# Gate and up weight forms of an fp32r feed-forward block at 28 different byte offsets in their places

## The chip, the cores and the metric

The kernel runs on one core of one Trainium2 chip. The metric is the device time of one execution in microseconds (us), smaller is better; for each kernel the median of its runs is given. The profile shows one execution, engine by engine: PE is TensorE's matmuls, PEld its weight loads (LDWEIGHTS, which overlap the matmuls), DVE is VectorE, ACT is ScalarE, POOL is GpSimd, SP is SyncE, which issues all the DMAs here.

## The reference

Input x has 2048 tokens of 512 features, all fp32. The result is x + s * g, with

```
xn = layernorm(x)
q, k, v = split(xn @ wqkv)                 # 32 heads of 16
phi(t) = where(t > 0, t + 1, exp(t)) + 1e-6
kv = sum over tokens of phi(k) v^T ; z = sum over tokens of phi(k)
s = ((phi(q) kv) / (phi(q) z + 1e-6)) @ wo
g = silu((gelu(xn @ w_gate) * (xn @ w_up)) @ w_down)
```

with w_gate and w_up 512 x 1792 and w_down 1792 x 512. The change touches how the weights of xn @ w_gate and xn @ w_up lie in SBUF.

## The kernel before, in words

Every fp32 product is made of three fp32r matmuls (mm3, lines 291 to 295): each operand is split into a high form, rounded to fp32r on ACT, and a low form, the rest, made on DVE (split, lines 287 to 289). Line 293 is stationary high by moving high, line 294 stationary high by moving low, line 295 stationary low by moving high. The PE therefore sees long rows of matmuls that each have 128 stationary columns, loaded by an LDWEIGHTS of their own, and 512 moving columns. The products are cut further by a seven-product scheme of the Strassen-Winograd kind: of each pair of 256-wide blocks seven products are made from sums of weights and sums of tokens (PRODUCTS, line 24).

The work has these stages in order of time: layernorm, transposes and the k and q products (to about 145 us of the span); the first half of the feed-forward, tokens 1024 and up (about 145 to 400 us, with kv and the matrix M made inside it and at its end); the attention output S, which is spread over the row of matmuls that follows; the second half of the feed-forward (to about 610 us); and the last products and outputs.

In the feed-forward there are 28 groups of weights, q = 0 to 27: 14 for the first half of the tokens and the same 14, prepared again, for the second; even q are gate blocks, odd q are up blocks. `prep_w(q)` (lines 687 to 709) loads a 512 KB block, forms sums of it on POOL (tmp) and writes 14 slices of 128 x 128 as high forms and 14 as low forms into one tile w of the pool "wp" (ACT writes the high ones, DVE the low ones). The pool has four places, used in turn (`sl = w_next[0] % 4`), each 28 x 128 fp32 numbers = 14,336 bytes in every partition. The places are used before that by the k and q weight forms KQ (line 346) and in between by the two forms M_hi and M_lo of the matrix M (lines 901 to 904). `fprod` (lines 713 to 723) multiplies: the stationary operand is a 128-column slice of w (tile names w), the moving one 512 columns of the token forms Xh or Xl (tiles of pool "xf", line 328). The seven products of a group go to PSUM tiles FX, FY and FZ, 42 matmuls in a group, 1,176 in all. The down products (tiles d, line 785 on) take token forms hh and hl as stationary operand and down-weight forms dwh and dwl as moving one; they do not read w.

The order of the work is written out by a planner (class Plan): PE's order is a list of keys made by hand, and each of the other engines' orders follows from costs and due times given in the code. It knows nothing of addresses. Pools are laid out in SBUF one after another: constants, xf, wp, rawp, dp, up, sm. In the built program before the change, xf starts at byte 5,248 of each partition, wp at 62,592, and the two SBUF operands of every matmul stand at a distance that is a multiple of 512 bytes.

Of the kernel before, what the change touches and what calls it, by code (L numbers as in the profile page):

```python
# [9 lines left out]
F32R = mybir.dt.float32r  # L10
# [4 lines left out]
P = 128  # L15
# [179 lines left out]
def kernel(  # L195
# [35 lines left out]
    def tile_in(pool_name, unit, shape, dtype, name, parts=1):  # L231

        gen = gens[pool_name, unit] = Gen(gens.get((pool_name, unit)))
        kept = []

        def get():
            if not kept:
                kept.append(pools[pool_name].tile(shape, dtype, name=name, tag=f"{pool_name}{unit}", bufs=1))
            return kept[0]
        return View([Res() for _ in range(parts)], get, gen, pool_name == "ps")  # L240
# [3 lines left out]
    def ring(tag, places):  # L244
        n = count[tag] = count.get(tag, -1) + 1
        return places[n % len(places)]
# [24 lines left out]
    def ext(ap):  # L271
        return View((), lambda: ap)

    def dma(dst, src, kb, name=""):
        do("SP", 0.1, lambda o, i: nc.sync.dma_start(o, i), dst, src, lat=2.3, kb=kb, name=name)
# [7 lines left out]
    def tt(eng, op, dst, a, b, n, name=""):  # L283
        e, c = (nc.vector, dve(n)) if eng == "DVE" else (nc.gpsimd, pool(n))
        do(eng, c, lambda o, p, q: getattr(e, f"tensor_{op}")(o, p, q), dst, a, b, name=name)  # L285

    def split(hi, lo, src, n, name="", eng="DVE"):
        copy("ACT", hi, src, n, name + "h")
        tt(eng, "sub", lo, src, hi, n, name + "l")
# [52 lines left out]
    def raw_tile(i, name, shape):  # L342
        return tile_in("rawp", i, shape, F32, name, 2)
# [255 lines left out]
    for n in range(NP):  # L599
# [5 lines left out]
        for i in range(2):  # L605
# [3 lines left out]
            if n < CL:  # L609
                if i:  # L610
                    b = tile_in("up", 19 + n, [P, 2, 2, P], F32R, f"b12_{n}", 2)
# [71 lines left out]
    ws = {}  # L683
# [3 lines left out]
    def prep_w(q):  # L687

        u, i = divmod(q % NQ, 2)
        rname = ring("raw", [R0, R1])  # L690
        raw = raw_tile(rname, f"raw{q}", [P, KT, 2 * P])
        dma(raw, ext((up_k if i else gate_k)[:, :, u * 2 * P:(u + 1) * 2 * P]), 512)
        sl = w_next[0] % 4
        w_next[0] += 1
        w = ws[q] = tile_in("wp", sl, [P, 2, 14, P], F32R, f"w{q}", 4)
        tmp = raw_tile(TMP, f"tmp{q}", [P, 8, P])

        def t(i, n=1):
            return tmp.part((tmp.res[i // 2],), (slice(None), slice(2 * i, 2 * (i + n))))
        a11, a21 = raw[:, 0:2, 0:P], raw[:, 0:2, P:]  # L700
        a12, a22 = raw[:, 2:4, 0:P], raw[:, 2:4, P:]
        tt("POOL", "add", t(0), a21, a22, 256, "S1")
        tt("POOL", "sub", t(1), t(0), a11, 256, "S2")
        tt("POOL", "sub", t(2), a11, a21, 256, "S3")
        tt("POOL", "sub", t(3), a12, t(1), 256, "S4")
        for g, src in enumerate((raw[:, :, 0:P], a22, t(0, 2), t(2, 2))):
            n = (GROUPS[g].stop - GROUPS[g].start) * P
            hv, lv = (w.part(w.res[g:g + 1], (slice(None), hl, GROUPS[g])) for hl in range(2))
            split(hv, lv, src, n, f"w{g}")
# [103 lines left out]
    def ffn(p, finish):  # L813
        base = 0 if p else NQ
        todo = [list(g) for g in groups]
        for u in range(NU):
            for i in range(2):
                q = base + 2 * u + i
                if q not in ws:
                    prep_w(q)  # L820
                quad(q, p)
            prep_d(p, u)
            if todo[0][-1] == u:
                g = todo.pop(0)
                down(p, g, g is None or g[0] == 0, not todo, finish)
# [75 lines left out]
    for nm in ("M_hi", "M_lo"):  # L901
        sl = w_next[0] % 4
# [119 lines left out]
```

## Time and profile before

| | |
|---|---|
| time before, median of 2 runs | 638.58 us (637.63 to 639.53) |
| time of the profiled execution | 640.52 us |
| its span, first to last instruction | 638.8 us |
| granted TensorE clock, mean | 0.994 of full speed |
| matmuls in the trace | 2,772, each with its weight load |
| of them with w as operand | 1,176 |

The page of the profile shows the busy time of each engine, the span in 40 slices, the DMA queues, the chain of work that ended last, and groups of instructions by source line, engine, operation and tile, with count, busy time and mean duration of one. A matmul's duration in the trace is longer than the distance to the next one, since matmuls are pipelined: the distance between the starts of neighbours (the pitch) is what adds up to time. The timeline lists instructions with start, duration and the idle time before them; the view by windows gives, for stretches of the span, each engine's busy time and its number of instructions.

### The profile page before, as it was taken

How to read it: one execution, taken by the hardware profiler on the slowest of the kernel's cores; microseconds unless marked ns; L12 is line 12 of the kernel's file. 1: busy time of each engine (PE TensorE's matmuls, PEld its weight loads, DVE VectorE, ACT ScalarE, POOL GpSimd, SP SyncE). 2: the span in 40 equal slices, each digit the busy share in tenths (PEclk: the TensorE clock that was granted, in tenths of full speed). 3: DMA queues.
4: the chain of work that ended last, by engine and by line, in shares of the span. 5: the costliest groups of instructions: out<-in, count | busy, mean ns of one | idle time of the engine just before them, and what ended most of it. 6: DMA issues, size and time to landing. Idle time of an engine off the chain costs nothing.

```text
span 638.8 us, 7793 instructions
## 1 busy us (share of the span) xinstructions
PE 620.2 (97%) x2772; PEld 506.8 (79%) x2772; DVE 418.5 (66%) x634; ACT 323.2 (51%) x571; POOL 261.8 (41%) x253
## 2 busy tenths in 40 slices
PE   6999899999999999999999999999999999999995
PEld 5787678888888888888887788878888888888884
DVE  5889778768866664673266787866666537733564
ACT  5667577777765641561255132256656316612431
POOL 3552654445554652352016245455546403510144
PEclk8999999999999999999999999999999999999998
DMA  6248830105323211111149444773222201101154
GB/s 230 92 126 238 267 103 33 67 34 158 106 66 100 56 48 37 60 42 58 34 140 352 183 174 139 266 237 93 68 65 67 67 24 43 33 1 33 34 190 139
DMA packets 52439, 68.66 MB, mean 107 GB/s; under 512 B 2864, under 2 KB 31792, under 8 KB 52400
## 3 DMA queue, kind: packets, MB, share of 16 engines
q1 hardware_dynamic: 52400, 68.17, 33.0%
q8 instruction: 21, 0.34, 0.2%
q14 instruction: 18, 0.15, 0.1%
HBM read 49.28 MB, written 18.87 MB: 107 GB/s over the span
## 4 chain that ended last, share of the span: by engine, by line
PE 86%; DMA 4%; DVE 4%; ACT 2%; issue 1%; POOL 1%; SPq 0%; DVEq 0%; ACTq 0%; POOLq 0%
PE FX L293 8%; PE FX L294 8%; PE FX L295 8%; PE d L295 7%; PE d L294 7%; PE d L293 7%; PE FZ L294 4%; PE FZ L295 4%; PE FZ L293 4%; PE sps L295 2%; PE sps L293 2%; PE sps L294 2%; PE FY L294 2%; PE FY L295 2%; PE FY L293 2%; PE gps L294 2%
## 5 line engine op out<-in xcount | busy, mean ns | idle before, releaser
L763 POOL TENSOR_TENSOR h<-h,g 128x512 f32<-128x512 f32 x42 | 63.2, 1506 | 164.0 <-DVE h L285 163.8
L293 PE MATMUL FX<-Xh,w 128*128 128x512 f32 x224 | 87.6, 391 | 0.2
L293 PE MATMUL d<-dwh,hh 128*128 128x512 f32 x224 | 87.8, 392 | 0.0
L294 PE MATMUL FX<-Xl,w 128*128 128x512 f32 x224 | 87.2, 389 | 0.0
L295 PE MATMUL d<-dwh,hl 128*128 128x512 f32 x224 | 87.2, 389 | 0.0
L295 PE MATMUL FX<-Xh,w 128*128 128x512 f32 x224 | 87.2, 389 | 0.0
L294 PE MATMUL d<-dwl,hh 128*128 128x512 f32 x224 | 87.1, 389 | 0.0
L285 POOL TENSOR_TENSOR tmp<-raw 128x256 f32<-128x256 f32 x56 | 47.9, 856 | 85.1 <-DVE w L285 62.4
L801 DVE TENSOR_TENSOR acc<-acc,d 128x512 f32<-128x512 f32 (+1 forms) x49 | 32.9, 674 | 58.1 <-PE d L295 58.1
L279 ACT COPY fu<-FX 128x512 f32<-128x512 f32 x56 | 32.9, 587 | 58.9 <-PE FX L295 58.8
L285 DVE TENSOR_TENSOR hl<-h,hh 128x512 fp32r<-128x512 f32 x56 | 53.4, 974 | 4.6 <-ACT hh L279 4.4
L279 ACT CAST hh<-h 128x512 fp32r<-128x512 f32 x56 | 34.5, 620 | 41.7 <-PE d L294 21.7
L293 PEld LDWEIGHTS FX<-Xh,w 128*128 128x128 f32 x224 | 42.0, 188 | 10.2 <-ACT fu L279 1.5
L285 DVE TENSOR_TENSOR w<-tmp,w 128x512 fp32r<-128x512 f32 x56 | 41.4, 754 | 13.3 <-ACT w L279 13.3
L294 PEld LDWEIGHTS d<-dwl,hh 128*128 128x128 f32 x224 | 42.1, 188 | 8.9 <-issue 0.2
L293 PEld LDWEIGHTS d<-dwh,hh 128*128 128x128 f32 x224 | 42.1, 188 | 8.9 <-issue 0.2
L295 PEld LDWEIGHTS d<-dwh,hl 128*128 128x128 f32 x224 | 42.0, 188 | 8.7
L295 PEld LDWEIGHTS FX<-Xh,w 128*128 128x128 f32 x224 | 42.1, 188 | 8.7
L294 PEld LDWEIGHTS FX<-Xl,w 128*128 128x128 f32 x224 | 42.1, 188 | 8.6
L293 PE MATMUL FZ<-Xh,w 128*128 128x512 f32 x112 | 43.6, 389 | 0.0
L294 PE MATMUL FZ<-Xl,w 128*128 128x512 f32 x112 | 43.6, 389 | 0.0
L295 PE MATMUL FZ<-Xh,w 128*128 128x512 f32 x112 | 43.6, 389 | 0.0
(186 smaller groups left out, 1402.2 us busy)
## 6 DMA issues: line engine op xcount, KB each, us to landing
raw<-in_B_w_gate SPq DMA_DIRECT2D x14, 512.0 KB, 3.8
raw<-in_B_w_up SPq DMA_DIRECT2D x14, 512.0 KB, 3.8
draw<-in_B_w_down SPq DMA_DIRECT2D x14, 512.0 KB, 3.4
x<-in_A_x SPq DMA_DIRECT2D x16, 256.0 KB, 3.0
q_d<-qp SPq DMA_DIRECT2D x16, 256.0 KB, 2.0
q<-q_d SPq DMA_DIRECT2D x16, 256.0 KB, 2.8
xh_d<-Xh SPq DMA_DIRECT2D x4, 896.0 KB, 5.4
xl_d<-Xl SPq DMA_DIRECT2D x4, 896.0 KB, 7.4
```

Source lines behind the costliest of these rows:

```text
L279: do("ACT", act(n), lambda o, i: nc.scalar.copy(o, i), dst, src, name=name)
L285: do(eng, c, lambda o, p, q: getattr(e, f"tensor_{op}")(o, p, q), dst, a, b, name=name)
L293: nc.tensor.matmul(ps, wh, mh, start=start, stop=False, skip_group_check=on)
L294: nc.tensor.matmul(ps, wh, ml, start=False, stop=False, skip_group_check=on)
L295: nc.tensor.matmul(ps, wl, mh, start=False, stop=stop, skip_group_check=on)
L763: do("POOL", pool(NC), lambda o, i: nc.gpsimd.tensor_mul(o, o, i), h, g, name="h")
L801: do("DVE", dve(D // n), lambda o, i: nc.vector.tensor_add(o, o, i), acc[p, j][cl], ps[cl], name="acc")
```

## The change

The tile of a group becomes one flat row of 28 x 128 + 116 numbers (14,800 bytes), and the group's forms begin 4 x (q + 1) numbers, that is 16 x (q + 1) bytes, into it: 16 bytes for q = 0, 448 for q = 27. The view that the rest of the code sees has the shape it had before.

```
-        w = ws[q] = tile_in("wp", sl, [P, 2, 14, P], F32R, f"w{q}", 4)
+
+        off = 4 * (q + 1)
+        w = ws[q] = tile_in("wp", sl, [P, 28 * P + 116], F32R, f"w{q}", 4).map(
+            lambda ap: ap[:, off:off + 28 * P].rearrange("p (a b c) -> p a b c", a=2, c=P))
```

In the built program each place of wp takes 14,816 bytes (pools give out whole 32-byte units), 480 more than before. So places 1, 2 and 3 start 480, 960 and 1,440 bytes later, and the pools behind wp (rawp, dp, up, sm) 1,920 bytes later; xf does not move. Both programs hold the same instructions in the same order with the same waits on every engine; what differs is addresses, and line numbers below line 695, which are 3 higher after the change. Taken modulo 512 bytes, the distance from the token forms Xh and Xl to the weight forms is 0 for all 28 groups before. After the change it is 16 + 16q plus 480 for each place before the group's own: 16, 0, 496, 480, 80, 64, 48, 32, 144, 128, 112, 96, 208, 192 for q = 0 to 13 and 240, 224, 208, 192, 304, 288, 272, 256, 368, 352, 336, 320, 432, 416 for q = 14 to 27. For even q it is an odd multiple of 16, for odd q a multiple of 32. The KQ forms in places 1 to 3 (480, 448 and 416 modulo 512 from Xh and Xl), the pair M and pqT, and the operands in pool "up" that meet Xh, Xl or KQ change their distance too; the down products and the sums over tokens (gps) do not, since both their operands move together.

## The prediction

> **What bounds the kernel now.** I read the page first, then the groups of PE's instructions, then busy time by windows, the list of who PE waited for, and last the timeline, for the distance between single matmuls.
>
> ```profile
> span 638.8 us, 7793 instructions
> PE 620.2 (97%) x2772; PEld 506.8 (79%) x2772; DVE 418.5 (66%) x634; ACT 323.2 (51%) x571; POOL 261.8 (41%) x253
> PE   6999899999999999999999999999999999999995
> PEclk8999999999999999999999999999999999999998
> PE 86%; DMA 4%; DVE 4%; ACT 2%; issue 1%; POOL 1%; SPq 0%; DVEq 0%; ACTq 0%; POOLq 0%
> ```
>
> PE is busy from end to end at full granted clock, and the chain that ended last is 86% PE. The windows say how closely, in the two stretches that hold nearly all of the feed-forward:
>
> ```profile
> core 0: us, PE busy (x) PEld busy (x) DVE busy (x) ACT busy (x) POOL busy (x), PEclk, DMA share, GB/s
> 160.00:350.00 190.00, 189.95 (x838) 156.68 (x836) 114.54 (x156) 93.02 (x166) 78.34 (x76) 1.00 0.28 89
> 400.00:620.00 220.00, 219.85 (x978) 181.38 (x977) 128.84 (x184) 99.63 (x174) 82.18 (x77) 1.00 0.26 84
> ```
>
> In the first, 838 matmuls fill 189.95 of 190 us: 226.7 ns each, with no wait. What a matmul here gains or loses reaches the end of the kernel one to one; what other engines gain or lose does not, as long as PE stays fed. So the question is whether the addresses change those 226.7 ns. The matmuls that read w are these, 672 + 336 + 168 = 1,176 of them:
>
> ```profile
> L293 PE MATMUL FX<-Xh,w 128*128 128x512 f32 x224 | 87.6, 391 | 0.2
> L294 PE MATMUL FX<-Xl,w 128*128 128x512 f32 x224 | 87.2, 389 | 0.0
> L295 PE MATMUL FX<-Xh,w 128*128 128x512 f32 x224 | 87.2, 389 | 0.0
> L293 PE MATMUL d<-dwh,hh 128*128 128x512 f32 x224 | 87.8, 392 | 0.0
> ...
> L293 PE MATMUL FZ<-Xh,w 128*128 128x512 f32 x112 | 43.6, 389 | 0.0
> ...
> L293 PE MATMUL FY<-Xh,w 128*128 128x512 f32 x56 | 21.8, 389 | 0.0
> ```
>
> FZ and FY have three such rows each. The mean of one (389 ns) is its time through the pipeline, not the pitch; the pitch is read from starts in the timeline:
>
> ```profile
> 547.90 0.39 PE L293 MATMUL FY<-Xh,w 128*128 128x512 f32 x1
> ...
> 550.40 0.39 PE L295 MATMUL FX<-Xh,w 128*128 128x512 f32 x1
> ```
>
> These are 12 matmuls, so 2.50 us / 11 = 227 ns, in agreement with the window. The down products d, whose operands lie in quite other tiles, go at the same pitch; here are the first and the last of 22:
>
> ```profile
> 230.79 0.39 PE L293 MATMUL d<-dwh,hh 128*128 128x512 f32 x1
> ...
> 235.55 0.39 PE L293 MATMUL d<-dwh,hh 128*128 128x512 f32 x1
> ```
>
> 4.76 us / 21 = 227 ns.
>
> **The change, part by part.**
>
> *Instructions.* None is added, removed or moved, on no engine and no queue: order, waits and DMAs are those of before. No step has a new predecessor, so nothing can become late unless an instruction gets longer.
>
> *The matmuls with w.* Before, every operand pair of the program is a multiple of 512 bytes apart. So no row shows a pitch at another distance modulo 512. What can be read is whether the pitch holds a term that could depend on it. For the pure stream of 512 columns the nearest row is the plain fp32 product pm, each of whose four calls runs as two passes:
>
> ```profile
> L907 PE MATMUL pm<-mstuff 128*128 128x512 f32 x8 | 3.6, 592 | 0.0
> 358.13 3.59 PE L907 MATMUL pm<-mstuff 128*128 128x512 f32 x8
> ```
>
> Eight passes whose last takes 0.59 us give (3.59 - 0.59) / 7 = 429 ns of pitch. If a plain fp32 pass streams at half the fp32r rate (my assumption; it makes the two nearly commensurate), the bare stream is 429 / 2 = 214 ns, and the 227 ns hold 12 ns on top, though each of those passes has a weight load too. So about 12 ns of each fp32r matmul go with loading weights beside a stream at full rate. One reading is a meeting of the two reads in SBUF, which could depend on distance; another is a fixed cost of the swap, which could not. For the upper side, the nearest rows are matmuls just after a wait of PE, when load and stream stand in another phase to each other:
>
> ```profile
> 58.58 0.50 PE L293 MATMUL X<-kq,Xh 128*128 128x512 f32 x1 [0.24 <-ACT u L279]
> 58.92 0.40 PE L294 MATMUL X<-kq,Xh 128*128 128x512 f32 x1
> ...
> 60.31 0.39 PE L294 MATMUL Y<-kq,Xh 128*128 128x512 f32 x1
> ...
> 61.23 0.39 PE L295 MATMUL Y<-kq,Xl 128*128 128x512 f32 x1
> ...
> 62.59 0.39 PE L295 MATMUL Z<-kq,Xl 128*128 128x512 f32 x1
> ```
>
> From 58.92 to 60.31 six pitches take 1.39 us, 232 ns each; from 61.23 to 62.59 six take 1.36 us, 227 again. So the term isn't a constant of the instruction: it moves by 5 ns on average with phase, and then locks. The first pitch here, 0.34 us, holds a late load; as nothing delays loads in the change, I don't take it as an end.
>
> The bounds for the 1,176 matmuls with w are then 214 and 232 ns: 1,176 x (214 - 226.7) = -14.9 us, and 1,176 x (232 - 226.7) = +6.2 us. Between them I take 226.7, so 0. The reason is the row that it is nearest to: the pitch is the same for FX, FY, FZ and d, whose tiles lie in many different places, and it comes back to 227 ns after each disturbance; a lock that is found again from any phase may be found again from any distance, which shifts the phase of the lines read as a late start does. This is an argument, and no measurement at another distance stands behind it.
>
> The Trainium skill, "TensorE: Matmul & The Clock Gate", section "Part 2: What happens when you issue a matmul", says that PE has two independent SBUF read ports, and that loading the next weights takes no read bandwidth from the running matmul; by it the distance is worth nothing, 0 us. The same page's section "Wait — 56ns, not 53.3ns?" gives 215.7 ns for the warm pitch at 512 columns; the trace's 226.7 differs by 11.0 ns, and if that were a collision that the shift removes, an estimate by the page's figure is 1,176 x 11.0 = 12.9 us saved. The page's two statements together leave the 11 ns unexplained, and no run here shows yet which gives way.
>
> *The other matmuls whose distance changes.* With KQ, M, and tiles of "up" against X: X 144, Y 36, Z 72, k 48, q 48 and sps 192, together 540 of 512 columns. By the same two bounds they are worth 540 x (-12.7) = -6.9 us to 540 x 5.3 = +2.9 us; taken 0 for the same reason. In the first stage PE also waits now and then, so part of either end would be lost in waits. The d and gps products keep their distances: 0.
>
> *Writing and reading w on ACT and DVE.* The forms now start 16 bytes off a 32-byte unit in even groups. No row of before has such a tile, so I bound by the cover.
>
> ```profile
> L279 ACT CAST w<-raw x56: 390/507/626, 136.6 to 554.1; 128x512 fp32r<-128x512 f32 x28, 128x256 fp32r<-128x256 f32 x28
> L279 ACT CAST w<-tmp x56: 604/617/627, 143.0 to 558.8; 128x512 fp32r<-128x512 f32 x56
> L285 DVE TENSOR_TENSOR w<-raw,w x56: 410/681/1517, 137.4 to 557.2; 128x512 fp32r<-128x512 f32 x28, 128x256 fp32r<-128x256 f32 x28
> L285 DVE TENSOR_TENSOR w<-tmp,w x56: 676/684/1794, 145.2 to 559.6; 128x512 fp32r<-128x512 f32 x56
> L295 PE MATMUL FZ<-Xh,w x112: 388/389/389, 155.1 to 609.9; 128*128 128x512 f32 x112
> ```
>
> A group takes four such writes on DVE (about 0.68 us each, 2.7 us) and four on ACT (0.51 and 0.62 us, 2.3 us). On PE a group takes 42 matmuls and its share of the down products, 672 / 28 = 24, together 66 x 226.7 ns = 15.0 us; by the first window DVE is busy for 114.54 / 190 = 60% of that, 9.0 us, and ACT for 49%, 7.3 us. So DVE has 6.0 us and ACT 7.7 us to spare in a group. The last write starts at 559.6 us and the last matmul with w at 609.9 us, so the forms are also made well ahead. Writes 1.5 times as long would add 1.4 us on DVE, which is hidden: 0. The cover is gone when the writes take over 6.0 / 2.7 + 1 = 3.2 times as long; at 4 times it is 8.1 - 6.0 = 2.1 us in a group, 28 x 2.1 = +59 us. Below 0 it can't be, since a shorter write has nobody waiting for it on PE.
>
> *Sum.* 0 + 0 + 0 against the profiled execution's 640.5 us (span 638.8 and 1.7 around it). That execution is 1.9 us above the median of the two runs, 638.58, of which the higher is 639.53; the median is what I carry over: **638.6 us**.
>
> **The rivals.**
>
> *Slower: other distances meet more often.* If the 12 ns are meetings of load and stream in SBUF, and the distance 0 modulo 512, with both starting together, is a good one, then the 27 groups that leave it pay. For it speaks that the pitch can be 232 for six matmuls in a row in another phase; against it that PE locks back to 227. At 232 ns in all matmuls with w it is +6.2 us, 644.8; with the 540 others +9.1 us, 647.7; at twice that surplus +18 us, 657. A loss of 2% (12.8 us) needs 12.8 / 1,176 = 10.9 ns on average on each matmul with w, or a pitch of 238 ns; from there it decides against "no change".
>
> *Faster: the old distance is the bad one.* All operands a multiple of 512 bytes apart and load and stream started together would be the worst case of a scheme that spreads addresses over banks, and the constant 12 ns its price. Then 27 of 28 groups (one comes back to 0 modulo 512) gain up to 12.7 ns: 1,134 x 12.7 = 14.4 us, 624.2; if half of the distances gain, 631.4; with the 540 others at best about 617. For it speaks that the surplus appears in every fp32r matmul and that all of them share the distance; against it that load and stream run on different addresses of moving rows, so that a shift by a few lines need not part them, and that phase, which does the same, made it only worse in the rows above.
>
> *Slower: the forms are written more slowly* on ACT or DVE off a 32-byte unit. From 3.2 times on it decides; 59 us at 4 times. Nothing in the profile speaks for so large a factor.
>
> **How the numbers follow.** About 2% is what a measurement of this kernel can tell from no change: 12.8 us, so faster is below 625.8 and slower above 651.4.
> - No dependence that adds up, my forecast: chance 0.56, 636 to 641.5 us, all within 2%.
> - More meetings: 0.24, spread from 642 to 660 and beyond; 0.11 of it above 651.4, 0.05 above 655.
> - Fewer meetings: 0.16, from 617 to 635; 0.05 of it below 625.8.
> - Slow writes: 0.04, all above 655.
>
> So faster 0.05, slower 0.11 + 0.04 = 0.15, within 2% 0.80. The range from 626 to 655 leaves out 0.05 below and 0.05 + 0.04 above, 0.14 together; the likeliest case's own range is 636 to 641.5.
>
> **What would show it.** Right: in the first window still about 838 matmuls in 190 us with PE waiting for nothing, the pitch 227 ns in groups of every distance, and w's writes on ACT and DVE at 0.62 and 0.68 us. Wrong: a pitch that differs from group to group while d keeps 227 ns (distance matters; the sign tells which rival), with even and odd groups apart if the 32-byte unit is what counts; a changed pitch of X, Z or sps; or PE waits on ACT w or DVE w, with those writes two or more times as long.

## The result and the profile after

The changed kernel takes 645.95 us (median of 2 runs, 645.88 to 646.03) against 638.58 before: a ratio of 1.0102, 95% interval 1.007 to 1.0135, so about 7.4 us or 1% slower. The two profiled executions, 640.52 and 646.03 us, differ by 5.5, since the one before was 1.9 us above its median. From the page of the profile after:

```profile
span 644.3 us, 7793 instructions
PE 628.2 (98%) x2772; PEld 507.5 (79%) x2772; DVE 421.1 (65%) x634; ACT 323.2 (50%) x571; POOL 261.5 (41%) x253
PEclk9999899999999999999999999999999999999999
L293 PE MATMUL FX<-Xh,w 128*128 128x512 f32 x224 | 88.7, 396 | 0.1
L294 PE MATMUL FX<-Xl,w 128*128 128x512 f32 x224 | 88.3, 394 | 0.0
L293 PE MATMUL d<-dwh,hh 128*128 128x512 f32 x224 | 87.8, 392 | 0.0
L295 PE MATMUL d<-dwh,hl 128*128 128x512 f32 x224 | 87.2, 389 | 0.0
```

PE is still the bound, with the same 2,772 matmuls and the same granted clock, and is 8 us longer busy. The groups show where: the matmuls with w went from 389 to 394 ns (391 to 396 in line 293), the down products d stayed at 389 to 392. The windows show that no wait came in; the columns are those of the same view before:

```profile
160.00:350.00 190.00, 189.96 (x826) 154.66 (x825) 112.76 (x153) 91.94 (x164) 76.54 (x75) 1.00 0.26 83
400.00:620.00 220.00, 219.90 (x966) 178.81 (x966) 127.09 (x183) 99.86 (x174) 80.55 (x77) 1.00 0.25 82
```

In the first stretch 826 matmuls instead of 838 fill the same 190 us. With 24 down products at 226.7 ns to 42 matmuls with w, 230.0 ns on average means about 232 ns for those with w. The timeline shows that it isn't the same for all groups. The first pair of lines is the first and last of 18 matmuls of group 2, at distance 496 modulo 512, the second the first and last of 17 of group 10, at distance 112:

```profile
171.97 0.39 PE L293 MATMUL FX<-Xh,w 128*128 128x512 f32 x1
...
175.83 0.40 PE L295 MATMUL FX<-Xh,w 128*128 128x512 f32 x1
...
282.72 0.39 PE L293 MATMUL FX<-Xh,w 128*128 128x512 f32 x1
...
286.45 0.39 PE L294 MATMUL FX<-Xl,w 128*128 128x512 f32 x1
```

3.86 us / 17 = 227 ns in the one, 3.73 / 16 = 233 ns in the other. Summing the distances between starts of all matmuls by output tile, FX, FY and FZ took 267.4 us before and 273.3 after, +5.9 us; all others together changed by -0.3 us. That makes +5.5, as the spans show.

The groups give a first map. At 0 and 496 the pitch is 227 ns, at 256 it is 227 wherever the row had settled, and at most other distances 230 to 234. Groups 256 bytes apart show the same patterns: at 80 as at 336 it goes 230, 235, 230, 235, at 112 as at 368 it stays at 233 and 234. One group will matter later: group 8, at 144 bytes, goes at 233.4 ns over its whole length. The writes of w did not change:

```profile
L279 ACT CAST w<-tmp x56: 602/617/628, 142.3 to 563.4; 128x512 fp32r<-128x512 f32 x56
L285 DVE TENSOR_TENSOR w<-tmp,w x56: 677/685/1786, 144.6 to 564.4; 128x512 fp32r<-128x512 f32 x56
```

The medians of 617 and 685 ns are within 1 ns of those before, although half of the groups lie 16 bytes off a 32-byte unit.

### The profile page after: what moved, and what is told of

The parts are those of the page before. It is cut to its first block, busy times and chain, and to the rows that moved or that the text cites. A ratio compares the mean times of both kernels' runs of the same rounds, so it can differ in the third digit from the quotient of the medians.

```text
span 644.3 us, 7793 instructions
## 1 busy us (share of the span) xinstructions
PE 628.2 (98%) x2772; PEld 507.5 (79%) x2772; DVE 421.1 (65%) x634; ACT 323.2 (50%) x571; POOL 261.5 (41%) x253
## 4 chain that ended last, share of the span: by engine, by line
PE 89%; DVE 4%; DMA 4%; ACT 2%; issue 0%; POOL 0%; SPq 0%; ACTq 0%; DVEq 0%
PE FX L293 8%; PE FX L294 8%; PE FX L295 8%; PE d L293 7%; PE d L294 7%; PE d L295 7%; PE FZ L294 4%; PE FZ L293 4%; PE FZ L295 4%; PE sps L293 2%; PE sps L295 2%; PE sps L294 2%; PE gps L294 2%; PE gps L295 2%; PE FY L294 2%; PE FY L295 2%
## 5 line engine op out<-in xcount | busy, mean ns | idle before, releaser
L293 PE MATMUL FX<-Xh,w 128*128 128x512 f32 x224 | 88.7, 396 | 0.1
L295 PE MATMUL FX<-Xh,w 128*128 128x512 f32 x224 | 88.2, 394 | 0.0
```

Of the source, the lines that this page charges most:

```text
L293: nc.tensor.matmul(ps, wh, mh, start=start, stop=False, skip_group_check=on)
L295: nc.tensor.matmul(ps, wl, mh, start=False, stop=stop, skip_group_check=on)
```

## The experiments

The theory to test was *distance*: the pitch of an fp32r matmul hangs on the distance, modulo 256 bytes, between the weights that are loaded and the tokens that stream. The rivals were *layout* (larger places, moved pools), *place* (where w lies by itself) and *alignment* (any step off the old grid). All times are compared with runs of the kernel before on the same chip, 638.7 to 639.0 us.

**pad_only: larger places, nothing shifted.**

```
-        w = ws[q] = tile_in("wp", sl, [P, 2, 14, P], F32R, f"w{q}", 4)
+        off = 0
+        w = ws[q] = tile_in("wp", sl, [P, 28 * P + 64], F32R, f"w{q}", 4).map(
+            lambda ap: ap[:, off:off + 28 * P].rearrange("p (a b c) -> p a b c", a=2, c=P))
```

> Places of the pool wp are 256 bytes larger, all forms begin at byte 0 of them; every operand pair stands at a distance that is 0 modulo 256 bytes (0 or 256 modulo 512). Theory distance (the pitch hangs on the distance between the weights that are loaded and the tokens that stream, with a period of 256 bytes, since in the changed kernel groups 256 bytes apart had the same pitch patterns): pitch 226.7 ns in all groups, time as before, 638.6 us within 1. Theory layout (larger places and pools that moved cost it): pitch 227 but some us more, up to the 7.4 us of the change. Theory 512 (the period is 512): the two groups of places in four at 256 go at 231 to 234 ns, +3 to +4 us.

639.2 us, ratio 1.0009 (0.9998 to 1.0019). From its windows:

```profile
160.00:350.00 190.00, 189.01 (x833) 155.88 (x831) 114.64 (x157) 92.65 (x165) 78.34 (x76) 1.00 0.28 89
```

189.01 / 833 = 226.9 ns, though half of the groups stand at 256 modulo 512. Larger places cost nothing, and 256 is as good as 0.

**all_96: all groups 96 bytes into their places.** As pad_only with `off = 24`.

> As pad_only, but all 28 groups begin 96 bytes into their places, a distance at which the changed kernel showed 234 ns. Theory distance: 234 ns in all groups, 1,176 x 7.3 ns = +8.6 us, about 647.2. If the 234 came from the change of distance from group to group, or from the first stage and M, which now stand at 0: 227 ns, about 638.6.

647.77 us, ratio 1.0139 (1.0115 to 1.0162): +9.0 us where +8.6 was expected. The mean pitch between matmuls with w is 234.2 ns. Its second window:

```profile
400.00:620.00 220.00, 219.95 (x961) 178.09 (x960) 126.45 (x182) 98.69 (x172) 80.86 (x77) 1.00 0.25 81
```

961 matmuls instead of 978 in 220 us, and PE is full: the time is in the matmuls, with all other pairs at 0.

**x_moved_96: the same distance, made by moving X.** As all_96, with 160 bytes more ahead of X, so that w is back at its old place modulo 256 and X has moved.

```
     ones = const("ones", [P, P])
+    pad = const("pad", [P, 40])
+    do("DVE", 0.1, lambda o: nc.vector.memset(o, 0.0), pad)
```

> As all_96, but everything behind the first constant moved by 160 bytes, so that the forms stand at the places modulo 256 bytes that they had before the change and the token forms X moved instead; the distance is 96 again, all other pairs at 0. Theory distance: as all_96, 234 ns and about 647.2 us. Theory place (the load is slower from addresses off 128 modulo 256): 227 ns, about 638.6.

647.5 us, ratio 1.0136 (1.0121 to 1.0151), mean pitch 234.2 ns. Group 5 runs through the same pitches as in all_96, number by number: 231, 234, 235, 234, 231, 238, 237, again and again. Place falls: w lies where it lay before the change, and the cost is that of all_96.

**low_96: the low weight forms alone moved by 96 bytes.**

```
+        w = ws[q] = tile_in("wp", sl, [P, 28 * P + 64], F32R, f"w{q}", 4).map(
+            lambda ap: ap[:, 0:28 * P + 48].rearrange("p (a b) -> p a b", a=2)[:, :, 0:14 * P]
+            .rearrange("p a (b c) -> p a b c", c=P))
```

> As pad_only, but the low weight forms alone stand 96 bytes further, the high ones at 0. Two of three matmuls then have weights at 0 (lines 293 and 294), one has them at 96 (line 295). Theory next load (the load of the next weights meets the stream that runs): the pitch from a 294 to its 295 grows by about 7 ns, the pitch from a 295 to the next 293 stays at 227; 392 x 7.3 = +2.9 us, 641.5. Theory own weights (a matmul is slower with its own weights at another distance): the pitch from 295 to 293 grows instead, the same time. If the lock as a whole is lost, all three grow, up to +8.6 us.

647.72 us, ratio 1.0132 (1.0096 to 1.0168), with the four runs spread from 644.3 to 649.4. The pitches after lines 293, 294 and 295 are 233.2, 231.6 and 232.7 ns: all three grow, the one after 294 least. One matmul in three at a bad distance takes the whole row out of its steady pattern; by the sum of starts the matmuls with w cost 6.6 us more, against 8.6 in all_96. Which two reads meet, this does not tell.

**probe: the map in steps of 4 bytes.** Extra rows of 14 matmuls (stationary `lo`, streaming `h`, 512 columns, nothing else on PE), ahead of the product z, whose bank they use.

```
+        def row(s, m, rows=P, n=14):
+            for _ in range(n):
+                nc.tensor.matmul(o[0:rows, 0:m.shape[-1]], s, m, start=True, stop=True)
+        for c in range(68):
+            row(lo[:, c:c + P], h)
+        for rows in (64, 32):
+            for c in (0, 24):
+                row(lo[:, c:c + rows], h, rows)
+        for cols in (384, 256):
+            for c in (0, 24):
+                row(lo[:, c:c + P], h[:, 0:cols])
...
+        for c in range(0, 68, 4):
+            row(b[:, 512 + c:512 + c + P], b[:, 0:512])
```

> The kernel before, with rows of 14 extra matmuls at one place in the middle (ahead of the product z, whose bank they use and which overwrites them), each row at one distance and with nothing else on PE between: 68 rows with the weights moved by 0, 4, 8, ... 268 bytes against 512 streaming columns; rows with 64 and 32 weight columns and with 384 and 256 streaming columns at 0 and 96 bytes; a row that alternates 0 and 96; and 17 rows in bf16 at steps of 8 bytes. The times of the whole mean nothing. Theory distance: 226.7 ns at 0 and 256 bytes (and at 240, 16 bytes before the period), 231 to 235 ns at the others, whatever the engines beside do. If the whole excess over the bare stream is a meeting of load and stream, fewer weight columns shorten it in proportion (64 columns: from 13 to about 7 ns at 0), and some distance under 16 bytes might go below 226.7; if the 13 ns at distance 0 are a fixed cost of the swap, they stay with 64 and 32 columns, and with 384 and 256 streaming columns. Bf16 moves half the bytes in the same time: by the meeting theory less excess or none, under 3 ns, with little dependence on distance.

From its timeline, merged, come the later matmuls of the rows at 0, 144, 212 and 256 bytes, then 64 and 32 weight columns (at 96 and 0 bytes), 384 streaming columns (at 96), 256 (at 0 and at 96), and bf16 at 8 bytes; the columns are start, time to the last one's end, and count:

```profile
343.20 2.66 PE L887 MATMUL pz<-zh,zl 128*128 128x512 f32 x11
...
460.25 2.66 PE L887 MATMUL pz<-zh,zl 128*128 128x512 f32 x11
...
515.16 3.00 PE L887 MATMUL pz<-zh,zl 128*128 128x512 f32 x12
...
550.70 2.90 PE L887 MATMUL pz<-zh,zl 128*128 128x512 f32 x12
...
567.04 2.66 PE L887 MATMUL pz<-zh,zl 128*64 128x512 f32 x11
...
570.00 2.94 PE L887 MATMUL pz<-zh,zl 128*32 128x512 f32 x12
...
578.99 2.07 PE L887 MATMUL pz<-zh,zl 128*128 128x384 f32 x11
...
581.50 1.24 PE L887 MATMUL pz<-zh,zl 128*128 128x256 f32 x9
...
582.70 1.69 PE L887 MATMUL pz<-zh,zl 128*128 128x256 f32 x13
...
594.57 2.54 PE L887 MATMUL pz<-bf 128*128 128x512 bf16 x11
```

With one matmul's own 0.39 us taken off (0.34 and 0.28 for the shorter streams, 0.38 in bf16) and divided by the count less one, the pitches are, to about 1 ns, 227, 227, 237, 228, 227, 232, 173, 120, 118 and 216 ns. The whole map, as the mean of the last nine pitches of each row, by distance in bytes:

```
  0: 226.7   4: 232.4   8: 230.7  12: 230.7  16: 233.6  20: 233.3  24: 231.1  28: 235.0
 32: 233.2  36: 234.6  40: 233.3  44: 229.6  48: 233.2  52: 233.3  56: 233.3  60: 230.1
 64: 233.0  68: 233.3  72: 233.3  76: 233.7  80: 231.7  84: 235.1  88: 233.3  92: 233.2
 96: 233.9 100: 226.7 104: 233.3 108: 230.1 112: 233.3 116: 233.3 120: 226.7 124: 231.9
128: 233.8 132: 228.1 136: 232.8 140: 233.4 144: 226.7 148: 233.0 152: 231.1 156: 226.7
160: 233.3 164: 235.2 168: 233.8 172: 235.6 176: 229.9 180: 232.9 184: 231.9 188: 233.3
192: 228.9 196: 233.0 200: 230.4 204: 226.7 208: 231.8 212: 236.4 216: 232.2 220: 233.4
224: 233.4 228: 226.7 232: 231.1 236: 231.7 240: 226.7 244: 226.7 248: 233.3 252: 226.7
256: 226.7 260: 232.4 264: 230.7 268: 230.7
```

Three things follow. The rows at 260, 264 and 268 run through the very pitches of 4, 8 and 12, one by one: the period is 256 bytes. The other engines have no part in it: from 470 to 590 us DVE, ACT and POOL did nothing, and the figures at 16, 96 and 112 bytes are those of the groups in the changed kernel. And for 128 weight columns and 512 streaming ones 226.7 ns is a floor, not one value among many: eleven distances reach it, none goes below. Steady rows of 512, 384 and 256 columns take 226.7 (at 0 bytes), 173.3 (at 96) and 120.0 ns (at 0), 53.3 ns per 128 columns and 13.4 ns over. But these 13.4 ns are not a floor for every shape: 256 columns at 96 bytes go at 117.6 ns, 2.4 below the steady row at 0. The excess does not shrink with the weights, although the loads do:

```profile
L887 PEld LDWEIGHTS pz<-zh,zl 128*128 128x128 f32 x1036 | 192.3, 188 | 43.0
L887 PEld LDWEIGHTS pz<-zh,zl 128*64 128x64 f32 x28 | 3.8, 134 | 2.6
L887 PEld LDWEIGHTS pz<-zh,zl 128*32 128x32 f32 x28 | 3.0, 108 | 3.4
```

With 64 weight columns the row still goes at 227 ns at 96 bytes and 229 at 0, with 32 columns at 230 and 232. That a part of the 13 ns is in proportion to the lines loaded has fallen. With 64 weight columns it is 96 bytes that settles at the floor, and 0 does not: which distances are good depends on the shape too, so the map is one for 128 by 512. A row that alternates 0 and 96 bytes goes at 230 ns on average, 229 and 231 in turn. In bf16 the pitch is 216 ns at all 17 distances (four gaps are twice that, where the trace lacks a matmul); there distance counts for nothing.

**all_144 and all_212: does the map hold in the kernel?** As pad_only with `off = 36` and `off = 53`.

> All 28 groups begin 144 bytes into their places, other pairs at 0. Theory distance, as the probe mapped it (226.7 ns at 144 bytes from the first matmul of the row on): 227 ns in all groups, time as before, 638.8 us within 1.5. Theory alignment (any shift off the old layout costs 5 to 8 ns, and the probe's rows without other engines at work don't carry over): 231 to 235 ns, 644 to 648.

639.39 us, ratio 1.001 (1.0 to 1.0021); mean pitch with w 227.5 ns. That mean hides two patterns. Most groups go at 226.6 to 226.7 ns throughout. But after short waits of PE, near the end of group 13 and in group 14, the matmuls with w went on in a cycle of 231 to 238 ns, stayed in it through groups 15 and 16, and came back to 226.7 in group 17, after a stretch of down products. Here are the first and the last of 39 matmuls in it:

```profile
441.98 0.40 PE L293 MATMUL FX<-Xh,w 128*128 128x512 f32 x1
...
450.85 0.39 PE L295 MATMUL FZ<-Xh,w 128*128 128x512 f32 x1
```

8.87 us / 38 = 233.4 ns, with the tiles, the distance and the stream's start of the rows at 226.7. It is also what group 8 of the changed kernel, at 144 bytes, showed. So one distance can have two steady patterns, and the row changed between them at breaks; by the sum of starts that cost 0.8 us here. In pad_only, at 0 and 256, every row came back to 226.7 after its breaks, within about a dozen matmuls.

> All 28 groups begin 212 bytes into their places, the distance with the longest pitch in the probe, 236.4 ns. Theory distance by the map: 1,176 x 9.7 ns = +11.4 us, about 650.2. Theory that any bad distance costs the same in the kernel: as at 96 bytes, +8.6 to +8.9, about 647.5.

650.49 us, ratio 1.0181 (1.0163 to 1.0199); mean pitch 236.4 ns, the probe's number. Its first window holds 814 matmuls for 838 before:

```profile
160.00:350.00 190.00, 189.96 (x814) 152.71 (x813) 109.94 (x150) 90.77 (x162) 74.75 (x75) 1.00 0.25 77
```

The map predicted both, 638.8 and 650.2, within 0.6 us. Alignment falls: 144 bytes off the old grid is nearly as good as 0.

**places_480: the change without the shift of w against X.** Places as in the change, `off = 8 * sl`.

> The change without its part: places and pools where the change puts them, but each group's forms begin 0, 32, 64 or 96 bytes into its place, so that weights and tokens stand at 0 or 256 modulo 512 again. KQ against X, M against pqT and the pairs with tiles of the pool up keep the distances of the change. Theory distance in the 1,176 alone: back to 638.8 within 1, since the other stages summed to about 0 between the two traces. If the places of the other tiles carry the rest of the 7.4 us: up to +1.5 us.

639.99 us, ratio 1.0016 (1.0004 to 1.0028): about 1.2 us of the change (0.3 to 1.8 by the interval) come from the other pairs and the moved places, the rest from the 1,176 matmuls.

**x_100: X itself 100 bytes further.** A try at a layout that settles faster.

```
-            XT[hl] = tile_in("xf", hl, [P, 14, NC], F32R, f"X{hl}{gen}", 0)
+            XT[hl] = tile_in("xf", hl, [P, 14 * NC + 64], F32R, f"X{hl}{gen}", 0).map(
+                lambda ap: ap[:, 25:25 + 14 * NC].rearrange("p (a b) -> p a b", b=NC))
```

> The kernel before with Xh and Xl each 100 bytes further into a place of 256 bytes more: weights with w stand at 156 bytes from X, X as weights at 100 bytes from KQ, both at 226.7 ns in the probe from the first matmul on, where the row at 256 took four matmuls to settle. Theory distance: 227 ns with w, time as before. If settling after a wait is faster at these distances, the first stage and the rows after transposes gain up to about 348 x 4 ns = 1.4 us: 637.4 to 638.8.

654.03 us, ratio 1.0235 (1.0216 to 1.0254): the expectation failed. Here are the first and the last of 18 matmuls with w in its timeline:

```profile
262.84 0.40 PE L293 MATMUL FY<-Xh,w 128*128 128x512 f32 x1
...
266.92 0.40 PE L295 MATMUL FX<-Xh,w 128*128 128x512 f32 x1
```

4.08 / 17 = 240 ns, steadily, at a distance that the probe had at 226.7. What differs from the probe is that here the streaming tile starts 4 bytes off a 16-byte line.

**x_96_d156: the same distance from a start on a line.** X moved by 96 bytes (`24:24 + 14 * NC`) and w by 252 (`off = 63`).

> As x_100, where the 1,176 went at 240 ns against my expectation, but X is moved by 96 bytes instead of 100 and w by 252, so that the distance from X to w is 156 again and X starts on a 16-byte line. Theory stream line (a streaming operand that starts off a 16-byte line costs 13 ns more, whatever the distance): 227 ns, about 638.8 us, perhaps 1 more from the first stage, where X stands at 96 from KQ. Theory distance 156 is bad in the kernel, unlike in the probe: 240 ns and about 654.

641.16 us, ratio 1.0034 (1.002 to 1.0048); mean pitch with w 226.8 ns. So 156 bytes is a good distance in the kernel too, and the 13 ns of x_100 came from where the pair starts. Of the 2.2 us that remain, the first stage's X, Y and Z products (now at 96 bytes from KQ) carry 1.0 us by the sum of their pitches; the rest isn't settled. The last 12 matmuls with w are an exception: they run through 235, 231, 254, 267, 244, 229 ns, at the same addresses modulo 256 where all rows before them had settled at 226.7.

**probe_stream: the start of the stream, by itself.** Rows of 14 matmuls ahead of the first S, with M_hi streaming from byte 0, 4, ... and the weights still, moved along, or 156 bytes further.

```
+                def row(s, c):
+                    for _ in range(14):
+                        nc.tensor.matmul(o, hf[:, s:s + P], mf[:, c:c + D], start=True, stop=True)
```

> The kernel before with rows of 14 extra matmuls ahead of the first product S, whose bank they use: 512 columns of M_hi stream, starting 0, 4, ... 64 bytes into it. 17 rows with the weights at byte 0 (distance minus the start), 17 rows with weights moved along (distance 0), and 10 rows with weights 156 bytes further. The times of the whole mean nothing. Theory stream line: 240 ns in every row whose stream starts off a multiple of 16 bytes, at any distance; 226.7 ns in the rows at distance 0 and 156 that start on one. Theory 64 (the line of the stream is 32 or 64 bytes): 240 ns at a start of 16 and 48, or 32, as well. Theory distance alone: 226.7 ns in all rows at distance 0 and at 156.

From its timeline, the rows at distance 0 that start at byte 4, 16 and 32, then those at distance 156 that start at byte 4, 32 and 96:

```profile
428.77 2.78 PE L948 MATMUL sps<-M_hi,pqTh 128*128 128x512 f32 x11
...
438.53 2.73 PE L948 MATMUL sps<-M_hi,pqTh 128*128 128x512 f32 x11
...
451.55 2.70 PE L948 MATMUL sps<-M_hi,pqTh 128*128 128x512 f32 x11
...
483.99 2.75 PE L948 MATMUL sps<-M_hi,pqTh 128*128 128x512 f32 x11
...
496.50 3.32 PE L948 MATMUL sps<-M_hi,pqTh 128*128 128x512 f32 x13
...
503.72 2.66 PE L948 MATMUL sps<-M_hi,pqTh 128*128 128x512 f32 x11
```

That is about 239, 234, 231 (226 to 227 in its last three), 236, 244 and 227 ns. At distance 0 the rows repeat every 32 bytes of start: 4 and 36 run at 237.8 ns, 8 and 40 at 231.1, 16 and 48 at 233.3, 20 and 52 at 234.6, and 0, 32 and 64 settle at 226.7. So at one distance the start of the stream counts too, modulo 32 bytes; the weights' start moves along with it, so these rows can't tell whose start it is. The 17 rows with the weights still say the same: where the stream starts at 32 and 64 bytes, which makes the distance 224 and 192, they have the map's 233.4 and 228.9 ns, but at 16 (distance 240) 231.2 instead of 226.7, and at 60 (distance 196) 226.7 instead of 233.0. So the map holds for a stream that starts on a 32-byte unit. My theory of 240 ns in every row off a 16-byte line was too simple: they go from 226.7 to 238, and at distance 0 a start at 16 costs 7 ns while at distance 156 it costs none. The pair of x_100 itself, distance 156 and a start at 100, goes at 235 ns here and not at 240. Two rows fit neither rule: at distance 156, starts of 32 and 64 run through 254, 266, 245, 229, 235, 231 again and again, 243 ns on average, where 0, 96 and 128 settle at 226.7. This is the cycle that the last matmuls of x_96_d156 run through, from a start at 96 that otherwise settles at 226.7. So at distance 156, as at 144, there is more than one steady pattern, and the start alone need not be the cause of the two rows. What chooses the pattern stays open.

## Why the prediction was right, and where it was not

The time, 645.95 us, lies within the range of 626 to 655, and the change is within 2%, as forecast with a chance of 0.80. But the case that I called likeliest, no dependence on the distance (chance 0.56, 636 to 641.5 us), is not what happened. It was the first rival, other distances meet more often (0.24). That the time still lay within the range is owed to the width of the range, which had room for that rival, and not to the mechanism that I held likeliest.

- *What bounds the kernel*: right. PE has no wait in the first window before or after, and every nanosecond per matmul reached the end: 9.7 ns x 1,176 = 11.4 us was expected of all_212, and 11.8 came.
- *The matmuls with w, taken 0*: this step failed; they cost 5.9 us. Its ground was that a lock which is found again from any phase may be found again from any distance. The lock at 226.7 ns exists, but only at some distances: 11 of the 64 steps of 4 bytes modulo 256 reach it (0, 100, 120, 144, 156, 204, 228, 240, 244, 252 as means of the last nine pitches, 132 only at the end of its row). At the others the row falls into a longer cycle, and at 144 it can do so too. All tiles of the kernel before stood at multiples of 512 bytes, so the agreement of FX, FY, FZ and d, on which I leaned, was one distance seen four times and no evidence on the others.
- *The upper bound, 232 ns*: as a mean over the change it was nearly exact (232 by the window; +5.9 us by sums of starts, against the +6.2 of the rival). That is luck: it came from six matmuls at distance 0 on their way back to 227, and the groups of the change lie between 226.6 and 234.2. As an end for one distance it was too low: 236.4 at 212 bytes, and 240 with the stream off its line.
- *The lower bound, 214 ns*: never reached. I had put about 12 ns down to loading weights beside the stream, some of which might be a meeting in SBUF. The probe has an excess of 13 ns at every good distance; it does not fall with 64 or 32 weight columns, and only the row of 256 columns at 96 bytes is a little below it (117.6 ns, 11 over). For the shape of these matmuls the rival *faster* had no room: before the change, the steady row already ran at the lowest pitch of all 64 distances.
- *The two statements of the Trainium skill* ("TensorE: Matmul & The Clock Gate"): the section "Part 2: What happens when you issue a matmul" has the load of the next weights take no read bandwidth from the running matmul. The 0 us that I drew from it did not come: in fp32r the pitch grows by 0 to 10 ns with the distance between the two operands. Whether it is read bandwidth that is lost, no run shows. The 215.7 ns of the section "Wait — 56ns, not 53.3ns?" agree with the probe in bf16, 216 ns, and not with fp32r, 226.7 at best. So the 11 ns of my estimate were nothing that one of the 64 shifts removes.
- *The other 540 matmuls, taken 0*: with the moved places 1.2 us (places_480), inside their bounds of -6.9 to +2.9. The step fails here too: leaving out the gaps of 300 ns and more, the mean pitch of X went from 228.7 to 232.5 ns, of Z from 227.7 to 233.3 and of sps from 229.8 to 231.4.
- *Writes of w*: right, 617 and 685 ns as before, hidden.
- *What would show it wrong* named the sign that came: a pitch that differs from group to group while d keeps 227 ns. The changed pitch of X, Z and sps was another. Even and odd groups do not stand apart; 240 modulo 256, an odd multiple of 16, is good, 32, 64 and 96 are not.

What is shown: with the stream on a 32-byte unit, the cost follows the distance between the stationary and the streaming fp32r operand, modulo 256 bytes, whichever of the two is moved (at 96 bytes), and with idle engines beside; at 144 and at 156 bytes a row can also stay in a slower pattern. What is only argued: that the two reads meet in SBUF. The exact repetition of the cycles speaks for a fixed mechanism between load and stream, but low_96 did not tell which load meets which stream, and the fixed 13 ns have no cause shown.

## What to carry to other kernels

In fp32r, with 128 weight columns and 512 streaming ones, give both operands of a matmul the same place modulo 256 bytes and start the streaming one on a 32-byte unit. This distance is also the safest of the good ones tried in the kernel, since rows at 0 and 256 came back to 226.7 ns after every break, and rows at 144 did not. In this kernel the difference between distances is 0 to 10 ns on 227 per matmul, up to 12 us of 639. After a change of tile sizes or of the order of allocation, look at the pitch in the timeline and at the mean duration (389 ns against 394 to 402): a slower row with no wait on PE is a sign of addresses. And when all rows of a profile share one condition, their agreement says nothing about that condition.

## What the hardware showed that I had not expected

- An fp32r row of one distance settles into an exact, repeating cycle of pitches, and the same distance mostly gives the same cycle, in quite other tiles too (at 96 bytes in all_96, x_moved_96 and the probe; in the probe at 4 and 260). But it can have a second one: 226.7 and 233 ns at 144 bytes, within one run.
- The start of the streaming operand counts too, with a period of 32 bytes at distance 0: 226.7 ns at 0, 237.8 at 4, 233.3 at 16.
- The excess of an fp32r matmul of 512 columns over its stream is 13 ns at best, and fewer weight columns do not lower it; in bf16 the pitch is 216 ns at every distance tried.
